# Exponentials of the first two sequences in five tiles in turn instead of three

## The chip, the cores and the metric

The kernel runs on one core of a Trainium2 chip. The metric is the device time of one execution in microseconds (us). The engines are named as the profile names them: PE is TensorE's matmul side and PEld its weight loads, DVE is VectorE, ACT is ScalarE, POOL is GpSimd, SP is SyncE, which here only issues DMAs. Each engine works through its own list of instructions strictly in the order in which it stands, and waits at the head of the list for semaphores of the others.

## What is computed

Three steps follow each other: attention with a threshold, and two feed-forward layers. The reference, cut to what matters:

```python
# q, k, v: 4 sequences, 8 heads, 576 positions, 64 wide
scores = scale * np.matmul(q, k.transpose(0, 1, 3, 2))
thresh = np.max(scores, axis=-1, keepdims=True) - tau
scores = np.where(scores >= thresh, scores, -1000000000.0)
scores = scores - np.max(scores, axis=-1, keepdims=True)
attn = np.exp(scores)
attn = attn / (np.sum(attn, axis=-1, keepdims=True) + 1e-09)
x = np.matmul(attn, v)            # -> 2304 tokens x 512
...
h = x @ moe_w_in                  # 512 -> 2048
x = (h * np.clip(h + 3.0, 0.0, 6.0) / 6.0) @ moe_w_out
...
r = np.maximum(x @ moe2_w_in, 0.0)
out = (r * r) @ moe2_w_out
```

## The kernel before

**Attention** is cut into units, one for each pair of heads of a sequence (4 sequences of 4 units), and a unit into nine jobs: four blocks of 128 query rows for each head, and one job for the 64 rows left over of both. A job is written in `scores`, `soft1`, `soft2` and, five jobs later (`LAG`), `av`. Jobs are counted here from 0; the first two sequences, called plain in the code, are jobs 0 to 71. For one of these jobs:

- PE multiplies the scores into a tile `s` of PSUM (L291). There are three such tiles (`N_S`).
- DVE takes the row minimum `nm` of the negated scores (L301), and POOL adds tau to it for the threshold `thr` (L303).
- ACT writes exp of the whole block into a tile in SBUF (L311). For the plain sequences this is a tile `g`, of which there are three (`N_G`), shared with the hidden layer of the feed-forward. The two later sequences write to tiles `e`, of which there are two.
- DVE sets what is under the threshold to zero and sums the rows (L318). After this the `s` tile is free.
- ACT copies the result to 16 bits, into a tile `wpo` (L324); POOL subtracts the copy for the low part, in two pieces (L325, L326). After L326 the `g` tile is free. There are four `wpo` tiles (`N_W`), shared with the weights.
- SP issues a DMA that transposes the `wpo` tile into `pt` (L328). After its landing the `wpo` tile is free.
- PE multiplies with the values (L350), ACT scales the result into `os` (L354, L357).

Beside the jobs, ACT copies the next unit's keys and queries (`kf` L199, `q_pl` L206 and L208), scales its values (L259) and copies finished blocks (`xr` L380, and `x` L390 once for a sequence). DVE takes the largest value of the next unit's `vraw` for the scale (`am` L243), which needs that unit's load (L174) to have landed, and writes the low part of the values (L260).

**Feed-forward.** The units of the first two sequences run almost alone: `paced` starts the hidden layer (`hidden`, PE L711, ACT L715, L718 and L721 into tiles `g`) after 73 steps of attention. Its first weights are split by ACT L627, DVE L630 and L631, ACT L638 into `wpi`, before PE can start. From then on feed-forward of sequences one and two runs beside the attention of the later two sequences, and at the end feed-forward runs alone.

**What sets the order.** The program text is not the order on the engines. The kernel is built with a scheduler that plays a timeline through with its own idea of how long each instruction takes and writes each engine's list in the order in which it sees work become ready. Whether a tile is free is part of what it sees. So a change of the tiles can change the order on all engines.

Of the kernel before, what the change touches and what calls it, by code (L numbers as in the profile page):

```python
# [33 lines left out]
N_G, N_PT = 3, 7  # L34
# [5 lines left out]
def attention_moe_moe_kernel(  # L40
# [239 lines left out]
    def scores(j):  # L280
# [14 lines left out]
                nc.tensor.matmul(s[:, half, 0:HALF], lhsT=u.qs[sl][:, cs], rhs=u.ks[sl][:, kk, c], start=i == 0, stop=i == len(ops) - 1)  # L295
        j.s = s[:, :, 0:HALF]

    def soft1(j):
        j.nm = st.tile([P, 1], F32, name="nm")
        j.thr = st.tile([P, 1], F32, name="thr")  # L300
        nc.vector.tensor_reduce(out=j.nm, in_=j.s, axis=AX.XY, op=ALU.min)  # L301
        if j.u.plain:
            nc.gpsimd.tensor_tensor(out=j.thr, in0=j.nm, in1=tau_a, op=ALU.add)  # L303
        else:
            nc.scalar.activation(out=j.thr, in_=j.nm, func=AF.Identity, bias=tau_a)
        if j.u.plain:

            j.e = me.tile([P, 2, HALF], F32, name="g", bufs=N_G)
        else:
            j.e = at.tile([P, 2, HALF], F32, name="e", bufs=2)  # L310
        nc.scalar.activation(out=j.e, in_=j.s, func=AF.Exp, bias=j.nm, scale=-1.0)  # L311
# [144 lines left out]
    def run(us, all_jobs, stop):  # L456
        n = len(all_jobs)
        pr = None
        for i in range(n + LAG):
            if i < n:  # L460
                j = all_jobs[i]
                if j.first:
                    if pr is not None:
                        for _ in pr:
                            pass
                    pr = prep_steps(us[j.u.i + 1]) if j.u.i + 1 < stop else None
                scores(j)
                soft1(j)
# [449 lines left out]
```

## Time and profile before

| what | us |
|---|---|
| median of 3 runs | 1089.61 |
| lowest and highest run | 1087.5 and 1090.9 |
| the profiled execution's own time | 1089.7 |
| its span, from the first to the last instruction | 1087.9 |

Over the whole span PE is busy for 94%, ACT for 59%, DVE for 57% and POOL for 46%. These shares are means over stages that differ: attention of the first two sequences lasts until about 176 us, then the two kinds of work run side by side, and from about 750 us on feed-forward is alone. What this change can do is read from the first stage.

### The profile page before, as it was taken

The numbers are of one execution on the slowest core, as the hardware profiler recorded it, in microseconds if no ns is written. First come the engines' busy times: TensorE is split into PE (matmuls) and PEld (weight loads), VectorE is DVE, ScalarE is ACT, GpSimd is POOL, SyncE is SP. The second block draws the span as 40 slices with busy tenths as digits, with TensorE's granted clock in tenths as the row PEclk, the third lists the DMA queues.
The fourth block names the chain that finished last, engine by engine and source line by source line (L and its number), as shares of the span: only waits on it lengthen the run. The fifth ranks groups of instructions, "written<-read, shape, count | busy, mean of one in ns | idle before, by whom it ended". The sixth has DMA issues, their size and how long they took to land.

```text
span 1087.9 us, 23244 instructions
## 1 busy us (share of the span) xinstructions
PE 1020.8 (94%) x9232; PEld 817.9 (75%) x9232; DVE 620.9 (57%) x1286; ACT 645.5 (59%) x1118; POOL 503.5 (46%) x665
## 2 busy tenths in 40 slices
PE   6988886899999998999999999999999999999998
PEld 4766664777787786888888788788887778778776
DVE  6877886667765678656756667744351233222122
ACT  6988985888675657785756567764333224223222
POOL 6877886455663545364565445553221112222111
PEclk9999998999999999999999999999999999999999
DMA  9998998476873547375545477765322232323211
GB/s 254 193 177 163 182 178 215 141 250 176 205 206 88 171 114 203 74 206 125 167 124 152 114 153 156 158 156 129 135 78 79 84 113 95 95 81 122 78 40 44
DMA packets 255820, 154.34 MB, mean 142 GB/s; under 512 B 215520, under 2 KB 227808, under 8 KB 255712
## 3 DMA queue, kind: packets, MB, share of 16 engines
q1 hardware_dynamic: 254064, 152.34, 55.9%
q8 instruction: 72, 1.18, 0.5%
q10 hardware_dynamic: 1648, 0.52, 0.2%
q14 instruction: 36, 0.29, 0.1%
HBM read 84.15 MB, written 23.86 MB: 99 GB/s over the span
## 4 chain that ended last, share of the span: by engine, by line
PE 63%; DVE 10%; ACT 10%; DMA 10%; issue 4%; POOL 3%; SPq 0%; POOLq 0%; ACTq 0%; DVEq 0%
PE y L751 29%; PE hp L711 26%; DMA wd<-in_moe_w_out_dram 4%; DMA wd<-in_moe_w_in_dram 3%; PE s L295 3%; PE o L350 2%; DMA vraw<-in_v_dram 2%; ACT g L311 2%; DVE wc L636 2%; DVE nm L301 2%; ACT wpo L324 2%; PE s L291 1%; DVE g L318 1%; ACT wc L627 1%; POOL wpo L326 1%
## 5 line engine op out<-in xcount | busy, mean ns | idle before, releaser
L711 PE MATMUL hp<-x,wpi 128*128 128x288 f16 x3072 | 397.4, 288 | 13.4 <-ACT wpi L638 6.8
L711 PEld LDWEIGHTS <-wpi 128*128 128x128 f16 x3072 | 298.4, 98 | 91.3 <-ACT wpi L638 7.4
L751 PEld LDWEIGHTS <-wpo 128*128 128x128 f16 x3072 | 298.4, 98 | 85.0 <-issue 5.7
L751 PE MATMUL y<-gh,wpo 128*128 128x288 f16 x2048 | 336.4, 288 | 8.5 <-DVE ya L757 3.3
L722 POOL TENSOR_TENSOR gl<-g,gh 128x576 f16<-128x576 f32 x128 | 165.2, 1293 | 356.0 <-ACT gh L721 354.3
L751 PE MATMUL y<-gl,wpo 128*128 128x288 f16 x1024 | 208.5, 287 | 0.2 <-POOL g L558 0.2
L757 DVE SCALAR_TENSOR_TENSOR ya<-y,yq,ya 128x576 f32<-128x576 f32 (+1 forms) x97 | 78.2, 809 | 100.0 <-PE y L751 99.7
L721 ACT ACTIVATE gh<-g 128x576 f16<-128x576 f32 x128 | 87.1, 681 | 62.0 <-DVE g L719 32.5
L301 DVE TENSOR_REDUCE nm<-s 128x1 f32<-128x576 f32 x144 | 107.9, 750 | 23.6 <-PE s L295 17.4
L718 ACT ACTIVATE g<-hp,r_w 128x576 f32<-128x576 f32 x64 | 47.0, 734 | 97.8 <-PE hp L711 97.7
L291 PE MATMUL s<-kf,q_pl 128*128 128x288 f32 x288 | 91.9, 447 | 12.9 <-DVE g L318 10.6
L350 PEld LDWEIGHTS <-pt 128*128 128x128 f16 x2016 | 78.9, 99 | 27.5 <-issue 17.4
L350 PE MATMUL o<-v,pt 128*128 128x64 f16 (+1 forms) x2016 | 87.0, 198 | 13.2 <-ACT xr L380 6.0
L719 DVE TENSOR_TENSOR g<-g,hp 128x576 f32<-128x576 f32 x64 | 48.0, 751 | 83.6 <-ACT g L718 83.5
L715 ACT ACTIVATE g<-hp,r_h,aq 128x576 f32<-128x576 f32 x64 | 52.8, 825 | 60.7 <-PE hp L711 60.4
L326 POOL TENSOR_TENSOR p<-e,p 128x512 f16<-128x512 f32 x72 | 85.0, 1180 | 0.0
L326 POOL TENSOR_TENSOR wpo<-g,wpo 128x512 f16<-128x512 f32 x72 | 84.4, 1172 | 0.0
L716 DVE SCALAR_TENSOR_TENSOR g<-g,r_w,hp 128x576 f32<-128x576 f32 x64 | 51.7, 810 | 55.2 <-ACT g L715 55.0
L318 DVE SCALAR_TENSOR_TENSOR e<-s,thr,e 128x576 f32<-128x576 f32 x72 | 58.4, 814 | 28.5 <-ACT e L311 27.9
L291 PEld LDWEIGHTS s<-kf,q_pl 128*128 128x128 f32 x288 | 53.0, 204 | 27.2 <-DVE g L318 9.5
L324 ACT ACTIVATE p<-e 128x576 f16<-128x576 f32 x72 | 49.1, 681 | 31.6 <-DVE e L318 23.6
L318 DVE SCALAR_TENSOR_TENSOR g<-s,thr,g 128x576 f32<-128x576 f32 x72 | 58.0, 810 | 12.0 <-ACT g L311 10.5
(129 smaller groups left out, 1167.1 us busy)
## 6 DMA issues: line engine op xcount, KB each, us to landing
wd<-in_moe_w_in_dram SPq DMA_DIRECT2D x16, 1024.0 KB, 7.2
wd<-in_moe_w_out_dram SPq DMA_DIRECT2D x16, 1024.0 KB, 6.8
wpi<-scr SPq DMA_DIRECT2D x32, 512.0 KB, 3.5
wpo<-scr SPq DMA_DIRECT2D x32, 512.0 KB, 3.7
scr<-wpi SPq DMA_DIRECT2D x16, 512.0 KB, 6.7
scr<-wpo SPq DMA_DIRECT2D x16, 512.0 KB, 6.1
kraw<-in_k_dram SPq DMA_DIRECT2D x16, 256.0 KB, 4.4
vraw<-in_v_dram SPq DMA_DIRECT2D x16, 256.0 KB, 3.3
```

Of the source, the lines that this page charges most:

```text
L291: nc.tensor.matmul(s[:, half, 0:HALF], lhsT=u.qf[:, t, :], rhs=u.kf[:, c], start=True, stop=True)
L301: nc.vector.tensor_reduce(out=j.nm, in_=j.s, axis=AX.XY, op=ALU.min)
L318: nc.vector.scalar_tensor_tensor(out=j.e, in0=j.s, scalar=j.thr, in1=j.e, op0=ALU.is_le, op1=ALU.mult, accum_out=u.sm[:, col:col + 1])
L324: nc.scalar.activation(out=p16[:, 0:S], in_=e, func=AF.Copy)
L326: nc.gpsimd.tensor_tensor(out=p16[:, S + TAIL:], in0=e[:, 0:NT * P], in1=p16[:, 0:NT * P], op=ALU.subtract)
L350: nc.tensor.matmul(o[:, n * w:n * w + w], lhsT=j.pt[:, c, :], rhs=vv[:, hs, vc, :], start=i == 0, stop=i == len(ops) - 1)
L711: last_hp[0] = nc.tensor.matmul(hp[:, a, 0:HALF], lhsT=wsl(seg, "i", f, w, c), rhs=x[c][:, a * HALF:(a + 1) * HALF], start=i == 0, stop=i ...
L715: nc.scalar.activation(out=g, in_=hv, func=AF.Relu, bias=r_h[:, q:q + 1], scale=seg.aq)
L721: nc.scalar.activation(out=gh, in_=gf, func=AF.Copy)
L722: nc.gpsimd.tensor_tensor(out=gl, in0=gf, in1=gh, op=ALU.subtract)
L751: nc.tensor.matmul(a[:, k_, 0:HALF], lhsT=wsl(seg, "o", f, w, e), rhs=g[f][:, k_ * HALF:(k_ + 1) * HALF], start=i == 0, stop=i == len(ops) ...
L757: nc.vector.scalar_tensor_tensor(out=y, in0=av_, scalar=yq, in1=y, op0=ALU.mult, op1=ALU.add)
```

## The change

A counter of all calls of `soft1` decides the tile: of each five exponentials of the plain sequences in turn three go to a `g` tile and two to an `e` tile. Both sets of tiles were there before, so no memory is added. For jobs 0 to 71 that gives 44 exponentials in `g` and 28 in `e`. The later sequences write to `e` as before.

```diff
+    n_soft = [0]
+
     def soft1(j):
...
-        if j.u.plain:
+        n_soft[0] += 1
+        if j.u.plain and n_soft[0] % (N_G + 2) < N_G:
 
             j.e = me.tile([P, 2, HALF], F32, name="g", bufs=N_G)
         else:
             j.e = at.tile([P, 2, HALF], F32, name="e", bufs=2)
```

No instruction is added or taken away: only the tile that an exponential writes to is another. But the order that the scheduler writes changes on all five engines: much from job 3 until the second sequence's attention is over, a little from there on. Behind the instruction that stands at 392 us in the trace of before, every engine's list is the same. Three places follow. Source lines behind `soft1` stand three lines lower in the changed kernel (L311 becomes L314, L324 becomes L327, L357 becomes L360, L318 becomes L321, L301 becomes L303). Numbers in names tell tiles apart.

**First place: jobs 55 to 58.** On ACT, before; `g_2304` is the exponential of job 56, `g_2350` of job 57, `g_2390` of job 58, and `wpo_2307<-g_2266` the copy of job 55:

```order
L311 ACTIVATE g_2304<-s_2297,nm_2300 128x576
L357 ACTIVATE os_2097<-o_2203,sm_1914 128x64
L354 ACTIVATE os_2097<-o_2237,sm_1914 64x64 x2
L199 ACTIVATE kf_2254<-tps_2255 128x256
L324 ACTIVATE wpo_2307<-g_2266 128x576
L357 ACTIVATE os_2097<-o_2276,sm_1914 128x64
L311 ACTIVATE g_2350<-s_2343,nm_2346 128x576
L324 ACTIVATE wpo_2353<-g_2304 128x576
L199 ACTIVATE kf_2254<-tps_2292 128x320
L311 ACTIVATE g_2390<-s_2383,nm_2386 128x576
```

On ACT, of the changed kernel, the same jobs:

```order
L314 ACTIVATE g_2304<-s_2297,nm_2300 128x576
L360 ACTIVATE os_2097<-o_2171,sm_1914 128x64
L360 ACTIVATE os_2097<-o_2203,sm_1914 128x64
L314 ACTIVATE e_2350<-s_2343,nm_2346 128x576
L357 ACTIVATE os_2097<-o_2237,sm_1914 64x64 x2
L199 ACTIVATE kf_2254<-tps_2255 128x256
L327 ACTIVATE wpo_2307<-g_2266 128x576
L327 ACTIVATE wpo_2353<-g_2304 128x576
L327 ACTIVATE wpo_2393<-e_2350 128x576
L360 ACTIVATE os_2097<-o_2276,sm_1914 128x64
L199 ACTIVATE kf_2254<-tps_2292 128x320
L314 ACTIVATE e_2390<-s_2383,nm_2386 128x576
```

Exponential and copy took turns before. Now exponentials run up to three jobs ahead and three copies follow in a row. Over jobs 0 to 71 there are 3 such bunches of three copies before and 13 in the changed order.

On DVE at the same jobs, before; `am_3711` is the largest value of the next unit, whose `vraw_3275` has to be loaded, and `g_2350` the cut of job 57:

```order
L301 TENSOR_REDUCE nm_2346<-s_2343 128x1
L318 SCALAR_TENSOR_TENSOR g_2266,sm_2268<-s_2259,thr_2263,g_2266 128x576
L318 SCALAR_TENSOR_TENSOR g_2304,sm_2268<-s_2297,thr_2301,g_2304 128x576
L334 RECIPROCAL sm_2268<-sm_2268 128x2
L243 TENSOR_REDUCE am_3711<-vraw_3275 128x1
L301 TENSOR_REDUCE nm_2386<-s_2383 128x1
L318 SCALAR_TENSOR_TENSOR g_2350,sm_2268<-s_2343,thr_2347,g_2350 128x576
```

On DVE, of the changed kernel:

```order
L303 TENSOR_REDUCE nm_2346<-s_2343 128x1
L260 SCALAR_TENSOR_TENSOR v16_2116<-vraw_1797,vsc_1367,v16_2116 128x640
L321 SCALAR_TENSOR_TENSOR g_2266,sm_2268<-s_2259,thr_2263,g_2266 128x576
L321 SCALAR_TENSOR_TENSOR g_2304,sm_2268<-s_2297,thr_2301,g_2304 128x576
L321 SCALAR_TENSOR_TENSOR e_2350,sm_2268<-s_2343,thr_2347,e_2350 128x576
L337 RECIPROCAL sm_2268<-sm_2268 128x2
L243 TENSOR_REDUCE am_3711<-vraw_3275 128x1
L303 TENSOR_REDUCE nm_2386<-s_2383 128x1
```

The cut (L318, L321 now) of job 57 moved from behind `am_3711` to ahead of it. On SP the load of `vraw_3275` stands behind the transpose of job 53 in both orders.

**Second place: from the first sequence to the second, jobs 26 to 31.** On DVE, before; `am_1717` needs the load of `vraw_1444`, `g_1205`, `g_1243` and `g_1291` are the cuts of jobs 28 to 30, `nm_1327` the minimum of job 31:

```order
L391 SCALAR_TENSOR_TENSOR x01_2944<-xr_561,sx_2937,x01_2944 128x576
L318 SCALAR_TENSOR_TENSOR g_1205,sm_1207<-s_1198,thr_1202,g_1205 128x576
L318 SCALAR_TENSOR_TENSOR g_1243,sm_1207<-s_1236,thr_1240,g_1243 128x576
L318 SCALAR_TENSOR_TENSOR g_1291,sm_1207<-s_1284,thr_1288,g_1291 128x576
L334 RECIPROCAL sm_1207<-sm_1207 128x2
L243 TENSOR_REDUCE am_1717<-vraw_1444 128x1
L301 TENSOR_REDUCE nm_1327<-s_1324 128x1
```

On DVE, of the changed kernel; `g_1127` is the cut of job 26 and `e_1159` that of job 27:

```order
L321 SCALAR_TENSOR_TENSOR g_1127,sm_848<-s_1120,thr_1124,g_1127 128x576
L337 RECIPROCAL sm_848<-sm_848 128x2
L260 SCALAR_TENSOR_TENSOR v16_1049<-vraw_731,vsc_179,v16_1049 128x640
L394 SCALAR_TENSOR_TENSOR x00_2941<-xr_561,sx_2937,x00_2941 128x576
L303 TENSOR_REDUCE nm_1155<-s_1152 128x1
L394 SCALAR_TENSOR_TENSOR x01_2944<-xr_561,sx_2937,x01_2944 128x576
L337 RECIPROCAL sm_848<-sm_848 128x2
L303 TENSOR_REDUCE nm_1201<-s_1198 128x1
L303 TENSOR_REDUCE nm_1239<-s_1236 128x1
L243 TENSOR_REDUCE am_1717<-vraw_1444 128x1
L321 SCALAR_TENSOR_TENSOR e_1159,sm_1207<-s_1152,thr_1156,e_1159 128x576
```

`am_1717` moved ahead by four cuts, and between the cut ahead of it and itself stand eight other instructions. On SP, its load stood behind the transpose of job 26 before, and stands behind that of job 23 and two loads of tails now.

**Third place: the end of the stage.** On ACT, before; `g_2888` is the exponential of job 71, `wpo_2891` and `wpo_2954` are the copies of jobs 70 and 71, `wc` and `wpi` the first weights:

```order
L311 ACTIVATE g_2888<-s_2881,nm_2884 128x576
L390 ACTIVATE x12_3148<-xr_1981,sx_3138 128x576
L357 ACTIVATE os_2770<-o_2802,sm_2616 128x64
L324 ACTIVATE wpo_2891<-g_2854 128x576
L357 ACTIVATE os_2770<-o_2865,sm_2616 128x64
L324 ACTIVATE wpo_2954<-g_2888 128x576
L357 ACTIVATE os_2770<-o_2897,sm_2616 128x64
L627 ACTIVATE wc_2837<-wd_2534,sp_2828 128x1024
L627 ACTIVATE wc_2913<-wd_2536,sp_2828 128x1024
L638 ACTIVATE wpi_2841<-wc_2837 128x1024
```

On ACT, of the changed kernel:

```order
L327 ACTIVATE wpo_2857<-g_2793 128x576
L360 ACTIVATE os_2770<-o_2865,sm_2616 128x64
L360 ACTIVATE os_2770<-o_2897,sm_2616 128x64
L314 ACTIVATE g_2888<-s_2881,nm_2884 128x576
L327 ACTIVATE wpo_2891<-g_2854 128x576
L630 ACTIVATE wc_2837<-wd_2534,sp_2828 128x1024
L630 ACTIVATE wc_2913<-wd_2536,sp_2828 128x1024
L327 ACTIVATE wpo_2954<-g_2888 128x576
L641 ACTIVATE wpi_2841<-wc_2837 128x1024
```

The last copy moved behind the two first steps of the weights.

## Rows read from the trace of the kernel before

**Rows 1.** Windows by stage: us, busy us per engine, instructions; clock, DMA share, GB/s.

```profile
12.40:175.70 163.30, 134.00 (x1344) 100.78 (x1342) 137.62 (x327) 145.77 (x317) 129.03 (x262) 0.96 0.99 189
...
181.00:392.00 211.00, 198.34 (x1733) 158.23 (x1734) 136.78 (x276) 145.27 (x219) 109.24 (x102) 0.99 0.61 176
392.00:1087.90 695.90, 682.43 (x6142) 555.07 (x6139) 339.20 (x669) 346.63 (x571) 254.24 (x269) 0.99 0.44 119
```

**Rows 2.** ACT by line, 12.4 to 175.7: busy us, mean ns; idle before.

```profile
L311 ACT ACTIVATE g<-s,nm 128x576 f32<-128x576 f32 x72 | 53.4, 742 | 11.0 <-DVE nm L301 4.3 <-POOL wpo L326 3.2 <-DVE sm L334 2.2
L324 ACT ACTIVATE wpo<-g 128x576 f16<-128x576 f32 x72 | 48.9, 684 | 4.7 <-DVE g L318 3.7 <-DMA pt<-wpo 0.5
L357 ACT ACTIVATE os<-o,sm 128x64 f32<-128x64 f32 x60 | 18.2, 315 | 1.7 <-PE o L350 1.3
L206 ACT ACTIVATE q_pl<-tps,qs 64x256 f32<-64x256 f32 x28 | 13.0, 466 | 0.3
L380 ACT ACTIVATE xr<-xT 128x256 f32<-128x256 f32 (+1 forms) x28 | 7.5, 295 | 0.7 <-PE xT L367 0.6
...
L199 ACT ACTIVATE kf<-tps 128x256 f32<-128x256 f32 (+1 forms) x14 | 5.7, 408 | 0.2
```

**Rows 3.** ACT's waits, 12.4 to 175.7: us in total, times, longest.

```profile
ACT g L311 <- POOL wpo L326: 3.2, 5, 1.8
...
ACT wpo L324 <- DMA pt<-wpo: 0.5, 2, 0.3
```

**Rows 4.** PE, DVE and POOL by line, 12 to 182.

```profile
L291 PE MATMUL s<-kf,q_pl 128*128 128x288 f32 x284 | 89.8, 443 | 12.9 <-DVE g L318 10.6 <-DVE sm L334 1.7 <-DVE ex L397 0.2
L326 POOL TENSOR_TENSOR wpo<-g,wpo 128x512 f16<-128x512 f32 x72 | 84.4, 1172 | 0.0
...
L325 POOL TENSOR_TENSOR wpo<-g,wpo 128x64 f16<-128x64 f32 x72 | 22.3, 310 | 14.1 <-issue 6.2 <-ACT wpo L324 2.9 <-POOL thr L303 2.3
...
L243 DVE TENSOR_REDUCE am<-vraw 128x1 f32<-128x640 f32 x9 | 7.4, 817 | 8.2 <-DMA vraw<-in_v_dram 7.0 <-POOL vraw L240 1.1
```

**Rows 5.** The transposes of line L328 until 180: issue's ns, then time to landing.

```profile
L328 SPq DMA_TRANSPOSE pt<-wpo x72: 1242/1333/3257, 16.5 to 178.8; - x72
...
DMA to landing us min/median/max: 3.2/3.7/7.2
```

**Rows 6.** Timeline of ACT and DVE, jobs 29 to 31: start, us, instruction, idle before.

```profile
75.97 0.74 ACT L311 ACTIVATE g<-s,nm 128x576 f32<-128x576 f32 x1 [0.73 <-POOL wpo L326]
...
78.98 0.74 ACT L311 ACTIVATE g<-s,nm 128x576 f32<-128x576 f32 x1 [1.80 <-POOL wpo L326]
...
82.57 0.82 DVE L243 TENSOR_REDUCE am<-vraw 128x1 f32<-128x640 f32 x1 [1.91 <-DMA vraw<-in_v_dram]
...
84.17 0.74 ACT L311 ACTIVATE g<-s,nm 128x576 f32<-128x576 f32 x1 [2.20 <-DVE sm L334]
```

**Rows 7.** Timeline of DVE and ACT around job 58.

```profile
143.69 0.82 DVE L243 TENSOR_REDUCE am<-vraw 128x1 f32<-128x640 f32 x1 [2.54 <-DMA vraw<-in_v_dram]
...
145.29 0.74 ACT L311 ACTIVATE g<-s,nm 128x576 f32<-128x576 f32 x1 [2.36 <-DVE nm L301]
```

**Rows 8.** Timeline of DVE and ACT around the copy of job 4.

```profile
22.69 0.87 DVE L260 SCALAR_TENSOR_TENSOR v<-vraw,vsc,v 128x640 f16<-128x640 f32 x1
...
24.39 0.68 ACT L324 ACTIVATE wpo<-g 128x576 f16<-128x576 f32 x1 [0.54 <-DVE g L318]
```

**Rows 9.** Timeline of ACT and PE at the end of the stage.

```profile
174.97 0.72 ACT L324 ACTIVATE wpo<-g 128x576 f16<-128x576 f32 x1
...
175.74 2.38 ACT L627 ACTIVATE wc<-wd,sp 128x1024 f32<-128x1024 f32 x2
...
181.03 1.14 PE L711 MATMUL hp<-x,wpi 128*128 128x288 f16 x4 [6.07 <-ACT wpi L638]
```

## The prediction

> **What bounds the kernel now.** I read the windows by stage first, since the mean over the span hides the stages. From 12.4 to 175.7 us, where the exponentials of the first two sequences stand, ACT is busy for 145.8 of 163.3 us, the most of all engines; DVE has 137.6, PE 134.0, POOL 129.0 [rows 1]. Behind 181 us it is PE: 198.3 of 211 us, and then 682.4 of 695.9. So the first stage goes at the pace of ACT, and what the change can give is some of ACT's idle time there: 163.3 - 145.8 = 17.5 us. ACT's work itself, the same instructions, stays.
>
> Then the groups of ACT and its waits, to see who makes that idle time. The wait that the extra tiles are meant for, an exponential that finds its `g` tile not yet read by POOL's L326, is 3.2 us in 5 of 72 cases [rows 2, 3]. That is little. The rest is spread: exponentials wait for the minimum `nm` (4.3) and once for DVE's `sm` (2.2), copies wait for the cut on DVE (3.7) [rows 2]. Of these the timeline tells that the two longest come from DVE standing at `am`, which waits for a load: 7.0 us in all [rows 4], 1.91 at 82.57 and 2.54 at 143.69, each followed by an ACT gap of 2.20 and 2.36 [rows 6, 7].
>
> **The change part by part.** No instruction is added, so every cost or gain is in who stands ahead of whom.
>
> *The tile waits.* The two large ones, 0.73 and 1.80, are at 75.97 and 78.98 [rows 6]. With five tiles the tile needed was free two jobs sooner. At both places the minimum was ready long before, so nothing else is late next for that exponential. I take all 3.2 us; the bounds are 3.2 and 0, if the three `s` tiles take over the wait (first rival).
>
> *From the first sequence to the second.* The gap of 2.20 at 84.17 is DVE's wait at `am_1717` passed on [rows 6]. In the new order this `am` stands ahead by four cuts, but its load ahead by three transposes, and eight DVE instructions now lie between the cut of job 26 and it. Two low parts of `x`, one of `v` and three minima among them are several us of work that covers the load. I take 1.9, the DVE wait itself; bounds 0 and 2.2.
>
> *Job 58.* The gap of 2.36 at 145.29 was DVE's wait at `am_3711` [rows 7]. In the new order the load stands at the same place on SP, and the wait may stay. But the cut of job 57 is now ahead of it, so on ACT three copies can fill the time: 3 x 0.684 = 2.05 us [rows 2], where one copy stood between the exponentials 57 and 58 before. I take 1.9; bounds 0.7 (one copy more) and 2.36.
>
> *Job 4.* Its cut stood behind the low part of `v`, 0.87 us, and the copy waited 0.54 for it [rows 8]; now the cut is ahead. I take 0.5.
>
> *The end of the stage.* Between the last copy and the first matmul of the hidden layer ACT, DVE and ACT again work on the first weights one after the other, and PE waits 6.07 for them [rows 9]. In the new order the first of these steps is ahead of the last copy, 0.72 us [rows 9]. Nobody waits for that copy soon: its transpose feeds a product that PE has behind the first hidden block. I take 0.7 from the path.
>
> Named gains: 3.2 + 1.9 + 1.9 + 0.5 + 0.7 = 8.2 us.
>
> *What the bunches cost.* This is the new wait. Copies write to four `wpo` tiles, and that number stays. In turns of exponential and copy, four jobs lie between a copy and the one that needs its tile. In 13 bunches of three now, where there were 3, the third copy of a bunch needs the tile of the second of the bunch before. For jobs 56 and 60 in the new order ACT has in between: 4 copies, 3 exponentials, 3 `os`, one `kf`, 3 `xr` and 2 `q_pl`, that is 2.74 + 2.23 + 0.95 + 0.41 + 0.89 + 0.93 = 8.1 us [rows 2]. In the same time POOL has to do job 55 and 56, 2 x (0.31 + 1.17) = 2.96, with one `sm` between them, behind the end of copy 55 [rows 4], and the transpose has to land, 3.7 at the median [rows 5]: 6.7, with the `sm` about 7.0. So the slack is 1.1 us where all goes well. A landing of 7.2, the longest [rows 5], makes it -2.4, and ACT would stand there, with the next exponentials queued behind the copy; DVE waits for these, and PE for the `s` tiles. Before, this wait was 0.5 us in all [rows 3]. The price of a bunch thus lies between 0 and 2.4 us. I take 0.25, near the median's end: 13 x 0.25 = 3.2 us.
>
> *Behind the stage.* Until 392 us the orders differ little and PE has 12.7 us of idle time in 211 [rows 1]. I take 0, give or take 1. Behind that the order is the same, and PE-bound; what is won by then stays won.
>
> Sum: 3.2 - 8.2 = -5.0. The profiled execution took 1089.7, of which 1.8 lie outside its span of 1087.9; it is 0.1 above the median of 1089.61. 1089.7 - 5.0 = **1084.7 us**.
>
> **The rivals.** *The three `s` tiles are the limit.* PE's scores wait 10.6 us for the cut on DVE that frees the `s` tile [rows 4], three times as long as exponentials wait for `g`. An exponential can't run ahead further than there are scores, so five tiles behind three would give nothing, the 3.2 would come back as a wait for the minimum, and the two `am` waits as well. Then 0.5 + 0.7 remain: 1089.7 - 1.2 = 1088.5, no measurable difference. For it: the 10.6. Against it: at the two `am` places it was DVE that was late, not the scores, and the changed order does run three exponentials ahead. The Trainium skill bears on this ("Perfetto Trace Analysis", Optimization Strategy): the same gap repeating on the engine that should be saturated can mean too few buffers in SBUF or PSUM. By that rule ACT's tile wait, 5 times in 72, is no sign of too few `g` tiles, and the repeating one is that for `s`, which the change leaves; by it the time would be that 1088.5.
>
> *The bunches cost more than is won.* The mechanism is the one above: the third copy stands at the head of ACT's list until a transpose has landed. At p us a bunch the time is 1089.7 - 8.2 + 13p. From p = 0.38 it is no longer faster by a measurable amount, from p = 0.88 it is slower; at 0.9 it is 1093.2. For it: the landing spreads from 3.2 to 7.2 and one issue took 3.26 where the median is 1.33 [rows 5], and the DMA share of this stage is 0.99 [rows 1], so three transposes in a row meet busy DMA engines. Against it: bunches that hold query copies have more ACT work between them than the one reckoned here.
>
> That the change does nothing can be left out: the changed order shows 28 exponentials written to `e`.
>
> **How the numbers follow.** Three runs of this kernel agree within about 0.3%, 3.3 us, and less than that can't be told from no change. The forecast, a gain of over 3.3, has 0.57. The `s` tiles have 0.18, the bunches at 0.38 to 0.88 us each 0.13: within 0.3% together 0.31. Bunches at over 0.88 have 0.12. Range: at the lower end no bunch waits and a quarter of the other 17.5 - 7.5 = 10 us of idle time goes too: 1089.7 - 8.2 - 2.5 = 1079. At the upper end the bunches cost 0.75 each: 1089.7 - 8.2 + 9.8 = 1091.3. So 1079 to 1091.5, which leaves out most of the slower case and a little below.
>
> **What would show it right or wrong.** In the changed kernel's waits, exponentials waiting for POOL's L329 should be near 0. The gaps of ACT at the exponentials of jobs 31 and 58 should be under 0.5. Copies waiting for the transposes' landing should total about 3 to 4 us; over 8 would be the second rival. PE's first hidden matmul should start near 176 instead of 181.03, and the time from there to the end should be the same within 1 us; a larger change there would mean that I looked at the wrong stage. Exponentials waiting for `nm` at over 7 us would be the first rival.

## The result and the profile after

| kernel | median us | lowest to highest | runs |
|---|---|---|---|
| before | 1087.66 | 1082.27 to 1110.39 | 20 |
| changed | 1095.11 | 1087.83 to 1099.47 | 20 |

The ratio is 1.0058, with a 95% interval of 1.0043 to 1.0073: the changed kernel is slower, by some 6 us, where a gain of 5.0 was forecast, and its median lies outside the range. (The one run of 1110.39 us, in a slower state of the chip, doesn't enter the ratio; the plain quotient of the two medians is 1.0068.)

One thing is needed to read its trace: the profiled execution took 1087.83 us (span 1086.0), by chance the fastest of its twenty. A second profile of the same kernel took 1095.61 (span 1093.8). So the totals of single traces say little, but the first stage is alike in both. Windows of the changed kernel, in the columns of [rows 1]; the first ends at ACT's first step on the weights (175.7 before), the second begins at PE's first hidden matmul (181.0 before):

```profile
12.40:181.50 169.10, 138.40 (x1344) 103.75 (x1342) 138.53 (x322) 144.94 (x316) 127.78 (x260) 0.94 0.99 182
187.10:392.00 204.90, 195.88 (x1726) 157.62 (x1727) 138.72 (x275) 143.93 (x217) 109.18 (x102) 0.98 0.64 182
392.00:1086.00 694.00, 681.71 (x6149) 555.04 (x6147) 339.62 (x671) 346.98 (x572) 254.21 (x269) 0.99 0.45 120
```

The same stage in the second profile:

```profile
12.40:181.10 168.70, 136.43 (x1345) 102.48 (x1343) 138.38 (x322) 145.17 (x317) 128.31 (x260) 0.96 0.97 183
```

ACT has the same work to do, 144.9 and 145.2 us busy against 145.8, but is idle for 169.1 - 144.9 = 24.2 and 23.5 us, where it was 17.5 [rows 1]. ACT's waits in that stretch, of the first profile (us in total, times, longest):

```profile
ACT g L314 <- DVE nm L303: 4.5, 5, 1.3
ACT os L360 <- PE o L353: 4.2, 5, 2.4
ACT wpo L327 <- DMA pt<-wpo: 3.1, 5, 1.9
ACT wpo L327 <- DVE nm L303: 2.3, 1, 2.3
ACT xr L383 <- PE xT L373: 1.7, 2, 1.2
```

and of the second:

```profile
ACT wpo L327 <- DMA pt<-wpo: 5.1, 4, 1.9
ACT os L360 <- PE o L353: 3.6, 5, 1.4
```

One row of the first list has to be read again: a copy doesn't read `nm`. The copy that waits 2.3 us there, of job 54, starts 0.08 us after the transpose that frees its tile has landed, as every copy that waits for a landing does in both profiles; and in the second profile the same copy waits 1.93 us for a landing:

```profile
142.48 0.68 ACT L327 ACTIVATE wpo<-g 128x576 f16<-128x576 f32 x1 [1.93 <-DMA pt<-wpo]
```

So copies wait 3.1 + 2.3 = 5.4 us for landings in the first profile and 5.1 in the second. Nearly all of it stands at the third copy of a bunch, of jobs 20, 26, 54 and 60 in the first (4.8 us), 20, 54 and 60 in the second (4.9); the other bunches wait for no landing at their third copy.

The wait that the tiles were meant for, 3.2 us for POOL [rows 3], is gone from both. What came in its place is the wait of a copy for a transpose to land (0.5 before, 5.4 and 5.1 now) and the wait of ACT's `os` for PE's products with the values (1.3 before [rows 2], 4.2 and 3.6 now). Of the gaps that the prediction named, none is left at the exponentials of jobs 29 to 31 or at the copy of job 4, and 0.22 at most at job 58. Others stand elsewhere. Timeline of ACT (start, us, instruction, idle before):

```profile
26.10 0.74 ACT L314 ACTIVATE g<-s,nm 128x576 f32<-128x576 f32 x1 [1.55 <-DVE gm L565]
...
29.97 0.31 ACT L360 ACTIVATE os<-o,sm 128x64 f32<-128x64 f32 x1 [2.35 <-PE o L353]
...
60.67 0.68 ACT L327 ACTIVATE wpo<-g 128x576 f16<-128x576 f32 x1 [1.90 <-DMA pt<-wpo]
...
141.61 0.68 ACT L327 ACTIVATE wpo<-g 128x576 f16<-128x576 f32 x1 [2.32 <-DVE nm L303]
```

At 141.61 stands the copy of job 54, the third of the bunch ahead of the one shown above under "First place"; its wait is the landing just told. At the end of the stage (timeline of ACT and PE, to set beside [rows 9]) the first steps on the weights are ahead of the last copy, as the new order says, but they begin 5.8 us later:

```profile
181.52 2.31 ACT L630 ACTIVATE wc<-wd,sp 128x1024 f32<-128x1024 f32 x2
...
183.74 0.67 ACT L327 ACTIVATE wpo<-g 128x576 f16<-128x576 f32 x1
...
186.01 1.06 ACT L641 ACTIVATE wpi<-wc 128x1024 f16<-128x1024 f32 x1 [1.61 <-DVE wc L634]
...
187.12 1.14 PE L714 MATMUL hp<-x,wpi 128*128 128x288 f16 x4 [8.64 <-ACT wpi L641]
```

PE's first hidden matmul is at 187.12, and at 186.69 in the second profile, instead of 181.03. From weights to matmul it takes 5.6 us, 5.3 before: the 0.7 expected from the last copy's place isn't there either.

### The profile page after: what moved, and what is told of

Same layout as the page of the kernel before. It is cut to its first block, busy times and chain, and to the rows that moved or that the text cites. A ratio compares the mean times of both kernels' runs of the same rounds, so it can differ in the third digit from the quotient of the medians.

```text
span 1086.0 us, 23230 instructions
## 1 busy us (share of the span) xinstructions
PE 1022.0 (94%) x9232; PEld 820.2 (76%) x9232; DVE 624.4 (57%) x1286; ACT 644.2 (59%) x1118; POOL 504.4 (46%) x665
## 4 chain that ended last, share of the span: by engine, by line
PE 65%; DMA 10%; ACT 9%; DVE 8%; issue 4%; POOL 4%; SPq 0%; ACTq 0%; POOLq 0%; DVEq 0%
PE y L754 30%; PE hp L714 25%; DMA wd<-in_moe_w_in_dram 4%; PE o L353 3%; DMA pt<-wpo 3%; PE s L295 3%; PE s L291 2%; DVE nm L303 1%; ACT wpo L327 1%; DVE wc L639 1%; ACT wc L630 1%; DMA pt<-p 1%; POOL wpo L329 1%; ACT e L314 1%; ACT g L314 1%
## 5 line engine op out<-in xcount | busy, mean ns | idle before, releaser
L303 DVE TENSOR_REDUCE nm<-s 128x1 f32<-128x576 f32 x144 | 107.7, 750 | 30.7 <-PE s L291 16.3
L353 PE MATMUL o<-v,pt 128*128 128x64 f16 (+1 forms) x2016 | 89.2, 198 | 14.5 <-ACT os L360 6.0
L321 DVE SCALAR_TENSOR_TENSOR e<-s,thr,e 128x576 f32<-128x576 f32 x100 | 81.1, 814 | 32.7 <-ACT e L314 31.2
L314 ACT ACTIVATE e<-s,nm 128x576 f32<-128x576 f32 x100 | 73.0, 730 | 1.6 <-DVE nm L303 0.4
L327 ACT ACTIVATE p<-e 128x576 f16<-128x576 f32 x72 | 49.1, 682 | 28.9 <-DVE e L321 21.5
L295 PE MATMUL s<-k_st,q_st 128*128 128x288 f32 x320 | 62.7, 318 | 1.1 <-DVE e L321 1.1
```

The lines of the kernel that those rows point to most:

```text
L321: nc.vector.scalar_tensor_tensor(out=j.e, in0=j.s, scalar=j.thr, in1=j.e, op0=ALU.is_le, op1=ALU.mult, accum_out=u.sm[:, col:col + 1])
L353: nc.tensor.matmul(o[:, n * w:n * w + w], lhsT=j.pt[:, c, :], rhs=vv[:, hs, vc, :], start=i == 0, stop=i == len(ops) - 1)
```

## The experiments

Three tools are used in them. **An order that is held:** at the end of the kernel's function every instruction of an engine is tied to the one ahead of it in another kernel's list, by an edge that sets the order and adds no wait on the chip. So tiles and order can be changed apart from each other:

```diff
+    for ids in listed.values():
+        ahead = None
+        for n in ids:
+            i = traced.get(f"I-{n}")
+            if i is not None:
+                if ahead is not None:
+                    tc.add_manual_dep(i, ahead, no_sync, reason="order")
+                ahead = i.name
```

**Turns:** an exponential may be placed only behind the copy of two jobs before, so no bunch of three copies can form. **Six tiles for the copies:** in turn four `wpo` tiles and the two `p16` tiles of the later sequences. Each ratio is against the kernel before on the same chip, with its 95% interval; the medians of before were 1087.2 to 1088.8 us, and each of the other kernels ran 6 or 12 times.

### Tiles or order?

**five_order_before**: the five tiles, every list held in the order of before.

> Five tiles in turn, but every engine's list held in the order of the kernel before. Theory A, the new order costs and the tiles alone do not: the 3.2 us of waits for a g tile go, nothing else changes, so 0 to 3 us faster than before (ratio 0.997 to 1.000). Theory B, the tiles e themselves cost (where they lie, or what they collide with): 5 us or more slower than before (ratio 1.005), as with the whole change.

**three_order_after**: three tiles, in the changed kernel's order.

> Three tiles as before, but every engine's list held in the order of the changed kernel. Theory A: slower than before by at least as much as the whole change, 6 us, and by some more where an exponential that now stands early waits for one of three tiles, up to 15 us (ratio 1.006 to 1.014). Theory B: within 2 us of before (ratio 0.998 to 1.002), since no e tile is written.

**after_again**: the changed kernel once more, on the chip of these runs.

> The changed kernel once more, for a second trace and an interval on the chip of the three kernels below. Both theories: 6 to 8 us over the kernel before. The last copy of job 71 ends at 182 to 186 us of its trace, 175.7 before, and the first hidden matmul starts at 186 to 190, 181.0 before. If the loss is not in this first stage, the first hidden matmul comes at 178 to 183 and the time is lost behind it.

**five_turns**: the changed kernel with the rule of turns, otherwise in the scheduler's own order.

```diff
+    copies = []
...
-        nc.scalar.activation(out=j.e, in_=j.s, func=AF.Exp, bias=j.nm, scale=-1.0)
+        with ExitStack() as held:
+            if j.u.plain and len(copies) >= 2:
+                held.enter_context(tc.issue_after(copies[-1]))
+            nc.scalar.activation(out=j.e, in_=j.s, func=AF.Exp, bias=j.nm, scale=-1.0)
...
-        nc.scalar.activation(out=p16[:, 0:S], in_=e, func=AF.Copy)
+        copies.append(nc.scalar.activation(out=p16[:, 0:S], in_=e, func=AF.Copy).ins)
```

> Five tiles, and the scheduler writes its own order, but an exponential must stand behind the copy of the job two before, so that exponentials and copies take turns and no bunch of three arises. Theory A with the bunches as the cause: 0 to 4 us faster than before (ratio 0.996 to 1.000). Theory A with something else in the new order as the cause (where loads and products stand): 3 us or more slower (ratio over 1.003). Theory B: ratio about 1.005.

| kernel | exponentials' tiles | order | ratio | interval |
|---|---|---|---|---|
| five_order_before | 5 | of before | 1.0003 | 0.9987 to 1.002 |
| three_order_after | 3 | of the changed kernel | 1.007 | 1.0048 to 1.0092 |
| after_again | 5 | of the changed kernel | 1.0051 | 1.0032 to 1.0071 |
| five_turns | 5 | its own, no bunch | 1.0009 | 0.999 to 1.0029 |

The loss belongs to the order, not to the tiles. But the first row of the table says as much about the gain: with five tiles and nothing else changed the wait for POOL is gone, and the time is that of before. ACT's waits in the first stage of five_order_before:

```profile
ACT g L314 <- DVE nm L303: 5.3, 3, 3.8
ACT wpo L327 <- DVE e L321: 3.8, 4, 2.1
ACT e L314 <- DVE nm L303: 2.7, 2, 2.3
ACT wpo L327 <- DVE g L321: 1.9, 4, 1.0
```

Exponentials now wait 5.3 + 2.7 = 8.0 us for the minimum. To set beside it, before, are 4.3 and the 2.2 at 84.17 [rows 2, 6], which the view puts down to `sm` although an exponential reads `nm` and no `sm`: 6.5. Copies wait 3.8 + 1.9 = 5.7 us for the cut, 3.7 before. So 1.5 and 2.0 us more stand there, and the 3.2 came back in these two waits. PE's waits for a score tile, same kernel and stretch, show what stands behind:

```profile
PE s L291 <- DVE e L321: 6.3, 5, 2.4
PE s L291 <- DVE g L321: 5.7, 5, 2.6
```

They were 10.6 [rows 4] and are 6.3 + 5.7 = 12.0. And at jobs 29 to 31 (timeline of ACT and DVE, to set beside [rows 6]) the two gaps of 0.73 and 1.80 are gone, and the next has grown by 1.62:

```profile
75.42 0.74 ACT L314 ACTIVATE g<-s,nm 128x576 f32<-128x576 f32 x1
...
76.52 0.75 ACT L314 ACTIVATE g<-s,nm 128x576 f32<-128x576 f32 x1
...
82.80 0.82 DVE L243 TENSOR_REDUCE am<-vraw 128x1 f32<-128x640 f32 x1 [3.02 <-DMA vraw<-in_v_dram]
84.32 0.74 ACT L314 ACTIVATE g<-s,nm 128x576 f32<-128x576 f32 x1 [3.82 <-DVE nm L303]
```

Job 30's exponential ran 2.5 us sooner, and job 31's 0.15 later: `am` and its load did not come sooner, so DVE stood there for 3.02 instead of 1.91. Here it was the load, and not the score tiles, that the next exponential waited for.

### Is it the bunches, and through the copies' tiles?

**turns_first** and **turns_second** are five_turns with the rule for sequence one alone (`j.u.b == 0` in place of `j.u.plain`) or for sequence two alone (`j.u.b == 1`). The first leaves 11 bunches of three, the second 6.

> Five tiles; exponentials and copies held in turns in the first sequence only, so that of the bunches of three (13 in the changed kernel) nearly all that are left are in the second sequence, 11 now. If the loss goes with the number of bunches: 11/13 of 6 us, ratio 1.004 to 1.006. If it is lost in the first sequence or at the change to the second: ratio 0.999 to 1.002.

> Five tiles; turns in the second sequence only; 6 bunches of three are left, all in the first sequence. If the loss goes with the number of bunches: 6/13 of 6 us, about 2.8, ratio 1.002 to 1.004. If it is lost in the second sequence: ratio 0.999 to 1.001; if in the first: 1.005.

**five_six_order_after**: the changed kernel, its order held, with six tiles for the copies.

```diff
+    n_copy = [0]
...
-        if u.plain:
+        n_copy[0] += 1
+        if u.plain and n_copy[0] % (N_W + 2) < N_W:
             p16 = new_w("o").rearrange("p a b -> p (a b)")[:, 0:2 * S]
```

> Order of the changed kernel held on every engine, five tiles for exponentials, and six instead of four tiles for the copies (two of the later sequences' 16-bit tiles taken in turn). So no copy waits for a transpose's landing. Theory A1, a bunch's copies at the head of ACT's list wait for the landing and that is the loss: those waits (3.2 and 5.1 us in two traces of the changed kernel) go and the time falls by as much, to a ratio of 1.001 to 1.003 over before. Theory A2, the loss lies in the order as a whole, engines that stand for each other in turn (products for the bunched transposes, os for the products, scores behind the products): another wait takes the place, the ratio stays at 1.004 to 1.007.

**three_six_order_after**: the same order and six copy tiles, but three tiles for the exponentials.

> Order of the changed kernel held, three tiles for exponentials as before, six for copies. It completes the square of tiles under the new order: three and four gave 1.007, five and four 1.005, five and six 1.000. If copies' tiles alone decide: 1.000 to 1.002. If under this order both sets are needed, since exponentials that stand early wait for a g tile (8.1 us of such waits with three and four): 1.004 to 1.007.

| kernel | ratio | interval |
|---|---|---|
| turns_first | 1.0039 | 1.002 to 1.0057 |
| turns_second | 1.0035 | 1.0021 to 1.0048 |
| five_six_order_after | 1.0004 | 0.9988 to 1.0021 |
| three_six_order_after | 1.0089 | 1.0068 to 1.0109 |

five_six_order_after is the changed kernel, bunches and all, and it has lost the loss. Its window of the first stage, and its largest waits on ACT there:

```profile
12.40:175.70 163.30, 132.74 (x1344) 99.37 (x1342) 136.28 (x324) 144.88 (x317) 128.52 (x260) 0.98 1.02 188
```

```profile
ACT os L362 <- PE o L355: 3.9, 5, 1.7
ACT g L315 <- DVE nm L304: 2.8, 3, 1.3
ACT e L315 <- DVE sm L339: 2.0, 1, 2.0
```

No copy waits for a landing, and the stage is 163.3 us long, as before. So what the bunches cost is the wait of third copies for their tile. One gap came back: the 2.0 in the third row is the exponential of job 58, behind the same `am` as before [rows 7], where the changed kernel shows 0.22 at most. In the new order with three and five tiles for exponentials, four and six for copies, the ratios are 1.007 (3, 4), 1.0051 and 1.0058 (5, 4), 1.0089 (3, 6) and 1.0004 (5, 6): either set alone is too small for this order. With three and six (ACT's waits) it is POOL again that ACT waits for:

```profile
ACT g L313 <- POOL wpo L329: 7.3, 15, 1.3
ACT g L313 <- DVE nm L303: 5.4, 8, 1.3
```

The two halves of five_turns don't add up by their bunches: 11 cost 0.39% and 6 cost 0.35%, with intervals that overlap widely, so a price for each bunch can't be told from them. The waits for landings in their traces don't go by the count either: 2.2 us with 11 bunches, 6.5 with 6. And five_turns, without a bunch, still has 2.9 us of them at a ratio of 1.0009.

Two versions were meant to win: **turns_six**, with six copy tiles and the rule of turns, and **five_six**, with six copy tiles and the scheduler's own order.

> Five tiles for exponentials, six for copies, and turns by the rule that an exponential stands behind the copy of the job two before; the scheduler writes its own order. If waits for tiles (of either kind) were what holds the first stage, it is 2 to 5 us faster than before, ratio 0.995 to 0.998. If ACT's list is held by the engines in turn and not by tiles, ratio 0.999 to 1.003.

> Five tiles for exponentials and six for copies, and the scheduler writes its own order (in the sequence that it gives, three exponentials often stand ahead, but copies come one by one more often). If tiles are what was missing, 1 to 4 us faster than before (ratio 0.996 to 0.999); if they only undo what the bunches cost, ratio 0.999 to 1.002.

They gave 1.0022 (1.0005 to 1.0038) and 1.0015 (0.9998 to 1.0033). More tiles undo the loss; none of these kernels beats the one before.

### Why did the gains come to nothing?

In five_order_before the waits for a tile are gone, in five_six_order_after also the gaps at jobs 31 and 4, and nothing is won. First suspect: DVE's wait at `am` for a load, which took over the gap above. In **am_tails_order_before** and **am_tails_five_six_order_after** `am` is, for the units of the first two sequences, the largest of the tails alone, which are loaded earlier; the maximum leaves the other values out. The `am` ahead of job 58 belongs to the first unit of the third sequence, which the edit does not reach.

```diff
-        nc.vector.tensor_reduce(out=am, in_=vin, axis=AX.X, op=ALU.max, apply_absolute_value=True)
+        top = vtl[u.b].rearrange("p h d -> p (h d)") if u.plain else vin
+        nc.vector.tensor_reduce(out=am, in_=top, axis=AX.X, op=ALU.max, apply_absolute_value=True)
```

> Kernel before with its order held, but am, the largest value of the next unit, is taken over the tails of all heads, which were loaded long ago, and not over the unit's own vraw: DVE doesn't stand for that load any more (7.1 us of waits in the trace of before). It leaves the other values out of that maximum. Theory P, an idle gap of ACT that is taken away comes off the time: the gaps of 2.20, 2.36 and 1.31 behind these waits go, 3 to 6 us faster (ratio 0.995 to 0.997). Theory S, ACT is held by whatever is late next and most of a gap comes back elsewhere: 0 to 2 us faster (ratio 0.998 to 1.000).

> The same edit of am on top of five tiles for exponentials and six for copies in the order of the changed kernel, which stood at 1.0004 with 6.7 us of am waits. Theory P: 0.995 to 0.997. Theory S: 0.998 to 1.000. If only the new order, with three exponentials ahead, can use the time: here 0.995, and 0.999 in the old order.

Measured: 1.0007 (0.9993 to 1.0021) and 1.0014 (0.9992 to 1.0036). ACT's waits in the first stage of am_tails_order_before:

```profile
ACT g L312 <- DVE nm L302: 4.4, 3, 2.4
ACT g L312 <- POOL wpo L327: 3.4, 6, 1.8
ACT wpo L325 <- DMA pt<-wpo: 3.2, 3, 2.5
```

DVE's waits at `am` for loads fell from 7.0 us to 2.3, with 1.2 for the tails. The 2.3 are the `am` that the edit does not reach, and the gap at job 58 stays:

```profile
143.36 0.82 DVE L244 TENSOR_REDUCE am<-vraw 128x1 f32<-128x640 f32 x1 [2.34 <-DMA vraw<-in_v_dram]
144.96 0.74 ACT L312 ACTIVATE g<-s,nm 128x576 f32<-128x576 f32 x1 [2.38 <-DVE nm L302]
```

The gap at job 31 fell from 2.20 to 0.24, and the 1.31 went, 3.3 us in all. By theory P that would be a ratio of 0.997. But the stage is 163.1 us long, 163.3 before, and copies wait for a landing instead, 3.2 against 0.5. One wait on a transfer took the place of another. So the next suspect was the transfers as a whole, since their share of this stage is 0.99 [rows 1].

Four kernels cut them down. For jobs 0 to 71 five of the nine blocks of a tile are transposed, and PE multiplies with the high parts a second time where the low parts stood: these kernels leave the low parts out and count the high ones twice. PE, DVE, ACT and POOL have the same instructions: **half_order_before** (three tiles, order of before), **half_five_order_before** (five tiles, same order), **half_order_after** (changed kernel, its order) and **half_three_order_after** (three tiles in that order).

```diff
-        nc.sync.dma_start_transpose(out=j.pt, in_=p16)
+        if u.plain:
+            nc.sync.dma_start_transpose(out=j.pt[:, 0:NT + 1], in_=p16[:, 0:S + TAIL])
+        else:
+            nc.sync.dma_start_transpose(out=j.pt, in_=p16)
...
-                nc.tensor.matmul(o[:, n * w:n * w + w], lhsT=j.pt[:, c, :], rhs=vv[:, hs, vc, :], start=i == 0, stop=i == len(ops) - 1)
+                nc.tensor.matmul(o[:, n * w:n * w + w], lhsT=j.pt[:, c % (NT + 1) if u.plain else c, :], rhs=vv[:, hs, vc, :], start=i == 0, stop=i == len(ops) - 1)
```

> The kernel before, every engine's list held, but for jobs 0 to 71 the DMA transposes five of nine blocks of the wpo tile (the high parts and the tails), and PE reads those blocks twice: the low parts of the exponentials are left out of the product. PE, DVE, ACT and POOL do the same work. In the first stage the DMA share was 0.99, so a third theory is that transfers set its pace: then about 0.3 of the share becomes free, the next limit is ACT's 145.8 us of work plus what it waits for other reasons, the first hidden matmul comes at 170 to 177 instead of 181.0 and the ratio is 0.991 to 0.997. If the chain of cuts, minima and score tiles between DVE, PE and ACT sets it, the first hidden matmul stays at 180 to 182 and the ratio is 0.998 to 1.002.

> The same with five tiles for the exponentials, in the order of before. If transfers swallowed what the five tiles give, it now shows: 2 to 4 us below the same kernel with three tiles. If not, within 1.5 us of it, as with full transposes (1.0003 against the kernel before).

> The changed kernel with its order held and the halved transposes. The bunches' price as a wait for the landing: with landings at half the work, copies wait under 1 us in all for them instead of 3.1 to 5.1, and the kernel is within 0.15% of the halved kernel in the order of before. If the order itself costs, without the landing, it stays 4 us or more above that one.

> Three tiles in the order of the changed kernel, with the halved transposes. Here POOL's freeing of the exponentials' tiles is the price (8.0 us of waits with full transposes), and the landing hardly (1.0). Both theories of the bunches say: still 6 us or more above the halved kernel in the order of before. If transfers set everything, it comes within 2 us of it.

In these four the order differs a little from the one to be held: early in the first sequence one or two loads on SP, and one or two groups of scores on PE, changed places with their neighbours.

| kernel | ratio | interval | first hidden matmul, us |
|---|---|---|---|
| half_order_before | 0.9909 | 0.9887 to 0.9931 | 173.4 |
| half_five_order_before | 0.9907 | 0.9888 to 0.9927 | 174.1 |
| half_order_after | 0.9918 | 0.9894 to 0.9943 | 175.2 |
| half_three_order_after | 1.0036 | 1.0016 to 1.0055 | 188.5 |

Window of the first stage of half_order_before, to set beside [rows 1]:

```profile
12.40:168.20 155.80, 132.73 (x1344) 99.87 (x1343) 137.60 (x328) 144.93 (x318) 129.81 (x262) 0.98 0.74 141
```

Its largest ACT waits in that stretch, and behind them DVE's wait at `am`:

```profile
ACT g L311 <- POOL wpo L326: 3.8, 6, 1.3
ACT g L311 <- DVE nm L301: 2.4, 3, 1.4
ACT wpo L324 <- DVE g L318: 2.2, 3, 1.0
```

```profile
DVE am L243 <- DMA vraw<-in_v_dram: 1.6, 2, 1.1
```

Three things follow. **The transfers take part in the pace:** the same work on the engines is done in 155.8 instead of 163.3 us, with ACT idle for 10.9 instead of 17.5. What went is, above all, the wait behind `am`: DVE waits 1.6 us for loads there instead of 7.0, exponentials 2.4 for the minimum instead of 6.5, and no landing took its place. **They are not what swallowed the tiles' gain:** with light transfers five tiles again give nothing against three (0.9907 and 0.9909), though three wait 3.8 us for POOL. PE's wait for score tiles is there in both, as a sum over `g` and `e` 8.2 us with three tiles and 9.0 with five. Its row with three:

```profile
PE s L291 <- DVE g L318: 8.2, 9, 2.6
```

**The bunches' price is the landing:** with five tiles and the transposes landing 2.8 us after their issue at the median instead of 3.7, half_order_after has no wait of a copy for a landing, and it is 0.1% from half_order_before, within the intervals. With three tiles the same order costs 1.0036 - 0.9909 = 1.3% on top, though the DMA share is down to 0.66 there: that price is POOL's, and no transfer's. ACT's first waits there:

```profile
ACT g L311 <- POOL wpo L326: 8.8, 18, 1.3
ACT g L311 <- DVE nm L301: 7.1, 9, 1.3
```

## Why the prediction was wrong, step by step

**What bounds the kernel.** The place was right, what sets its pace only in part. With full transposes, where the kernels differ in time, most of it shows at PE's first hidden matmul, to within some 2.5 us:

| kernel | that matmul, us after 181.0 | excess of the ratio, us |
|---|---|---|
| am_tails_five_six_order_after | -0.8 | 1.5 |
| am_tails_order_before | -0.3 | 0.8 |
| five_six_order_after | 0.3 | 0.4 |
| turns_six | 0.3 | 2.4 |
| five_order_before, five_six | 1.3, 1.3 | 0.3, 1.6 |
| five_turns | 2.9 | 1.0 |
| turns_second, turns_first | 3.9, 4.8 | 3.8, 4.2 |
| after_again, changed | 5.7, 6.1 | 5.5, 6.3 |
| three_order_after | 6.8 | 7.6 |
| three_six_order_after | 7.2 | 9.7 |

(The excess is the ratio less one, times 1087.6.) I took ACT for the engine that sets the pace, and its idle time for what could be won. But lighter transfers took 6.6 us of that idle time away and five tiles took none.

**The tile waits, 3.2 us.** They vanished, and the step failed with "nothing else is late next for that exponential". That held for job 30, whose exponential did come sooner, and not for the one behind it, which waits for a minimum behind `am` and its load. It is measured alone in five_order_before: 1.5 us more of waits for the minimum, 2.0 more of copies for the cut, no gain. That is the return which the first rival foretold, but where it can be followed, at job 31, the cause is the load and not the rival's three score tiles. The rival's sign, over 7 us of waits for `nm`, couldn't tell the two apart. The views give 4.9 and 4.5 us of them in the changed kernel's profiles; with the exponentials whose wait is put down to `gm`, `vsc` or `sm` but ends with their minimum it is 7.2 and 8.1, and by the same count before it was 6.5.

**The gaps at jobs 31 and 58, 1.9 each, and at job 4, 0.5.** In the changed kernel the gaps went, as the order said they would. That of job 58 was only covered: with the copy of job 54 held for 2.3 or 1.9 us by a landing, DVE comes to `am` later and stands 0.6 or 0.8 us there; without that hold, in five_six_order_after, it stands 1.75 and the gap is back at 2.0. ACT's idle time of the stage did not go: 18.8 us in five_order_before, 18.4 in five_six_order_after, 17.5 before. I priced each gap by its length, and that is the step that failed most: none of them shortened the stage. In am_tails_order_before, where 3.3 us of gaps go in the old order and the stage keeps its length, that is seen by itself.

**The end of the stage, 0.7.** From the first step on the weights to the first hidden matmul the changed kernel takes 5.6 us instead of 5.3. Moving the copy off that stretch brought nothing.

So of the 8.2 us named as gains the runs show about none: with the bunches' price taken away, by more copy tiles, the new order gives 1.0004.

**The bunches, 3.2 us.** The mechanism is right, a third copy that waits for a landing, and the size was too small: copies wait 5.4 and 5.1 us for landings where I had said 3 to 4, and 0.5 before. The 3.1 of the first list looks like a hit only because one landing stands there under another name. The price by the ratios is 1.0051 or 1.0058 less 1.0004, that is 5 to 6 us, about what these waits grew by (4.6 to 4.9). On the mean of 13 bunches it is some 0.4 each, the second rival's p of 0.38; but it is not spread: three or four third copies wait, up to 2.3 us, and the others don't. By that rival's own sum it would still have been no slower than before, because it kept the 8.2 as won; the direction came out the other way through the gains that failed.

The Trainium skill, "Perfetto Trace Analysis", Optimization Strategy, reads the same gap repeating on the engine that should be saturated as a possible sign of too few buffers. The trace of the changed kernel agrees in part: the copies that wait for a landing, 4 to 6 of 72, did mean too few copy tiles for that order, and six of them brought the ratio from 1.0051 and 1.0058 to 1.0004. But five tiles where ACT had waited 3.2 us brought nothing (1.0003): a gap names the buffer that is waited for, not what the next wait will be.

**Behind the stage.** I wanted the time from the first hidden matmul to the end the same within 1 us, and that test was too narrow. It is 1087.9 - 181.0 = 906.9 us before, 1086.0 - 187.1 = 898.9 in the first profile of the changed kernel and 1093.8 - 186.7 = 907.1 in its second. The 8.2 us between the two arise ahead of 720 us; the last 2,800 matmuls of the feed-forward take the same time in both to 0.1 us. One place is between 260 and 280 us, in the first profile and in the second:

```profile
260.00:280.00 20.00, 18.82 (x158) 15.31 (x158) 17.02 (x36) 16.45 (x28) 11.08 (x11) 1.00 0.51 114
260.00:280.00 20.00, 18.37 (x133) 13.82 (x133) 14.48 (x34) 13.34 (x22) 8.95 (x10) 0.83 0.39 77
```

In the second the granted clock fell from its higher level (2.4 GHz) to its lower (1.2 GHz) for part of the stretch, 0.83 in the mean, and PE did 133 matmuls instead of 158. There PE had stood idle for 2.59 us, waiting for DVE; at the same place in the first profile it was 1.99, and the clock stayed.

**What stays open.** What holds the stage at about 163 us with full transposes, beside the transfers, was not pinned to one resource. The score tiles are a candidate, with PE waiting some 6 to 13 us for the cut that frees them in every trace; a fourth was not tried. Against them speaks five_six_order_after: its stage is as long as before, but PE waits 6.5 us for them instead of 10.6, and DVE 13.9 us for PE's scores instead of 5.2. Nor is it settled why the halved kernels gain about 3 us more than their first hidden matmul shows (9.9 against 7.6 us in half_order_before, where the interval of the ratio gives 7.5 to 12.3).

## What to carry to other kernels

A buffer count is also an input of the scheduler: hold the order and change the tiles, then hold the tiles and change the order, before either is credited or blamed. Price a gap not by its length but by what is late next behind it, and if a second set of tiles (here the copies') has to follow the deeper run-ahead, count its landing times with it. When waits move from place to place and the stage keeps its length, look for a resource that the waits have in common (here the transfers, as loads and as landings), and lighten it by itself. And ask of each row of waits whether the instruction reads what it is said to wait for.

## What the runs showed of the hardware

- Single executions of one kernel differ by some 8 us behind the first stage (898.9 and 907.1 us for the same instructions), more than the whole effect that was looked for; part of it comes with stretches at the lower granted clock (0.83 against 1.00 from 260 to 280 us). Medians of many executions could tell 0.5%, one trace couldn't.
- Waits for transfers change places until the transfers get lighter. With a DMA share of 0.99 ACT waited 0.5 us for landings and DVE 7.0 us for loads; fewer waits at `am` (2.3, and 1.2 for the tails) brought more for landings (3.2) and the same stage; taking four ninths of the transposed blocks away left 1.6 and none, at a share of 0.74, and shortened the stage by 7.5 us.
- The issue of a transpose hardly became shorter with its size: 1.33 us at the median for nine blocks [rows 5], 1.21 for five. The median time to landing went from 3.7 us to 2.8.
